# Linear attention and two experts on one core: inputs asked for earlier, finer dependencies in the plan, other buffers, another seam

## The chip, the cores and the metric

The kernel runs on one core of a Trainium2 chip. The metric is the device time of one execution in microseconds (us). Names: PE is TensorE, DVE is VectorE, ACT is ScalarE, POOL is GpSimd, SP is SyncE, whose queue issues the DMAs.

## What is computed

```python
def _attn_ref(q, k, v):                      # 4 x 8 heads x 768 x 64
    gamma = 1.0 - 2.0 ** (-5.0 - np.arange(H))
    for t in range(S):
        state = gamma * state + einsum('bhd,bhe->bhde', k[:, :, t], v[:, :, t])
        y[:, :, t] = scale * einsum('bhd,bhde->bhe', q[:, :, t], state)
# x: [3072, 512], the heads side by side
def _moe_ref(x, w_in, w_out, g_ln):          # 512 -> 1024 -> 512
    h = x @ w_in
    solu = h * softmax(h)
    return (layer_norm(solu) * g_ln) @ w_out
def _moe2_ref(x, w_in, w_out):               # 512 -> 2048 -> 512
    h = x @ w_in
    return (h * np.cos(h)) @ w_out
```

The weights come as 64-bit numbers and are turned into float32 on the chip. Nearly every product is made of three matmuls, because each operand is split into a high and a low part (high*high, high*low, low*high).

## The kernel before

**Plan and order.** `Body.record` doesn't issue instructions. It records operations with `Plan.add`: an engine, an estimated cost, a function that issues, keys that are read (`r`) and written (`w`), and a bias. An operation's due time is the PE work recorded before it, plus the bias. `Plan.order` then simulates the engines by these costs and keys. PE takes its operations in recorded order or out of a short look-ahead; DVE, ACT and POOL take the ready one that is due first; SP takes a ready one among the next 16 in due order that are due within `SP_WIN` = 10 us of the first (lines 180 and 181). A DMA's end is taken from its size over `MBUS` plus `LAND`. The order in which the simulation starts them is the order in which every engine's instructions are issued; on the chip each engine works through its own list in order. Two operations that write one key are put one behind the other by the plan, with the landing of a DMA between them, also where the tiles behind the key are different ones.

**Stage 1, to about 387 us.** 24 attention steps, each 64 tokens of two batches, each with one block of small 64x64 matmuls: scores of step n + 1 (`sc`, L325), the state (`S`, L333) and the outputs of step n (`y`, L346). `load` (L285) brings a step's inputs by two DMAs, `dk` (L292) and `sv` (L296), into three buffers each. `attend` in `record` records the load of step n + 1 ahead of the block with outputs n. Between the steps stand the first expert's matmuls: `mm1` (L603) with `norm`, then for groups of 512 tokens `transp` (L665) into two PSUM banks, whose high and low parts ACT and DVE write (`lth`, `ltl`), and `mm2` (L697). One unit of `mm2` is 24 matmuls into one bank; ACT copies the bank to `ys` (L708, one buffer), and SP stores that to DRAM (`y1d`, L713). The last `HOLD` = 2 units of the first five groups are kept back until the attention is over.

Beside this, `keep` prepares the second expert's weights in 16 blocks: raw words are fetched into one buffer (`raw0`, L422), ACT and DVE turn them (`words`, L429 to L449), ACT and DVE write high and low parts into one buffer `big`, and SP stores these to DRAM (`cbd`, L586, and `o2d`, L538).

**Seam, about 369 to 416 us.** The held units, then `SEAM`, an order written out by hand: the last group's transposes (`t:`), its `mm2` units in parts (`m:d:a:b`), and the first products of the second expert (`P:`). `load_y` fetches `y1d`, forms sums and writes high and low parts to `Y`; half 0 at step `Y_AT`, half 1 behind the attention.

**Stage 2, to the end.** Three superblocks of 1024 tokens. Each has a first loop of eight steps (7 products, L867, with weights `cb` in three slots, and the previous step's part of the output matmuls `acc`, L973) and a second loop of eight steps with `acc` alone. A product goes through `wave` (six ACT and DVE operations, cosine among them, `ki` in two buffers) to a `G`. Each of the 16 steps takes one pair of weight pieces `o2` (L808, 512 KB each), in three slots; the pair for step k + 3 is asked for behind step k. At the end of each loop `leave` copies four banks and issues eight output stores (L1003). `load_cb(q + 3)` is recorded behind the products of step q; `load_y(s + 1)` between the two loops. The buffers for Y's raw sums (`yts`) lie in part in the tile that the products' ACT copies use too.

Of the kernel before, what the change touches and what calls it, by code (L numbers as in the profile page):

```python
# [33 lines left out]
NS = NB2 * NI  # L34
# [3 lines left out]
HOLD = 2  # L38
NU = 10
RING = 4  # L40
# [11 lines left out]
MBUS = 0.40  # L52
EASE = 0.08
FETCH = 3.4
BACKLOG = 5.0
WARM = 28
V_ACT = (0, 1, 3, 4, 5, 6, 7)
LAND = 2.0
# [14 lines left out]
JOIN = 2  # L73
Y_AT = 21
B_YLOAD = 0.0
# [9 lines left out]
SEAM = ("t:0 t:1 P:1 P:2 t:2 t:3 P:5 t:4 t:5 P:6 m:0:0:1 t:6 t:7 P:7 m:0:1:3 P:4 m:0:3:4 P:3"  # L85
        " m:1:0:4 m:2:0:4 m:3:0:4")
# [24 lines left out]
class Plan:  # L111
# [115 lines left out]
class Body:  # L227
# [121 lines left out]
    def attn(self, scores=None, outs=None, look=1):  # L349
# [7 lines left out]
        if outs is not None:  # L357
# [8 lines left out]
            if i:  # L366
                r += [("s", n % 2), ("dk", n % 3)]
# [17 lines left out]
        if carry:  # L385
            def copy():
                s = self.new("att", ("s", n + 1), [128, 8, D], F32, f"s{(n + 1) % 2}")
                self.nc.scalar.activation(out=s, in_=self.t["S", self.steps[n][0]], func=AF.Copy)
            self.add("ACT", 0.62, copy, r=[("S",)], w=[("s", (n + 1) % 2)])
# [111 lines left out]
    def keep(self, what):  # L501
# [11 lines left out]
        rk, wk = self.words(what, src, "stg", 0, False, early=EARLIER)  # L513
# [13 lines left out]
        if not wk_in:  # L527
# [13 lines left out]
            for l in range(2):  # L541
                self.add("SP", 0.4, lambda l=l: store(l), r=[("big",), ("big", l)], w=[("o2d", it, l)], mb=0.524, bias=b + B_STORE)
# [38 lines left out]
        for i in range(2):  # L581
# [5 lines left out]
            self.add("SP", 0.4, store, r=[("big",)] + [("big", m) for m in range(3)], w=[("cbd", 2 * c + i, e)], mb=0.459, bias=b + B_STORE)  # L587
# [130 lines left out]
    def load_y(self, s, es=(0, 1)):  # L718
        T, nc = self.t, self.nc
        for e in es:  # L720
# [11 lines left out]

            def yt(e=e):
                return T["yts", e]

            def fetch(m, e=e, yt=yt):
# [5 lines left out]
            def split(k, a, b, x, y, old=[], e=e, tile=tile, pools=pools, yt=yt):  # L742
# [13 lines left out]
                r = [("yt", e, i) for i in range(x, y)]  # L756
                self.add("ACT", 1.10 if b - a > 1 else 0.62, high, r=r + pools, w=[k, (*k, a)] + old, bias=B_YMIX)
                self.add("DVE", 1.25 if b - a > 1 else 0.70, low, r=r, w=[k, (*k, a)], bias=B_YMIX, name="two")
            for m in range(2):
                self.add("SP", 0.4, lambda m=m, fetch=fetch: fetch(m), r=[("y1d", 2 * s + m, 2 * e + i) for i in range(2)] + pools,  # L760
                         w=[("yt", e, 2 * m), ("yt", e, 2 * m + 1)], mb=0.524, bias=B_YLOAD)
# [3 lines left out]
            for to, x, y in ((0, 2, 0), (2, 3, 2), (3, 3, 0), (1, 1, 3)):  # L765
                self.add("DVE", 0.70, mix(to, x, y), r=[("yt", e, x), ("yt", e, y)], w=[("yt", e, to)], bias=B_YMIX, name="two")
# [3 lines left out]
    def load_cb(self, q):  # L770
# [21 lines left out]
        if sl != 1:  # L792
            self.add("SP", 0.5, fetch, r=r, w=[("cb", sl)] + old, mb=1.835, bias=B_CB)
        else:
            for e in range(2):
                for l in range(2):
                    self.add("SP", 0.4, lambda e=e, l=l: fetch(e, l), r=r, w=[("cb", sl)] + (old if not e + l else []),
                             mb=0.459, bias=B_CB)

    def load_o2(self, k):  # L800
# [8 lines left out]
        for l in range(2):  # L809
            self.add("SP", 0.4, lambda l=l: fetch(l), r=[("o2d", it, l)],  # L810
                     w=[("o2", sl)] + ([("u", 8), ("u", 9)] if k == 0 and l == 0 else []), mb=0.524, bias=B_O2)

    def rooms(self):
# [3 lines left out]
        def stg():  # L817
            T["yts", 1] = self.p["stg"].tile([128, 4, 512], F32, tag="raw0", name="yts")
            T["kis"] = self.p["stg"].tile([128, 2, 512], I32, tag="wt0", name="kis")
        self.add("CTL", 0.0, stg, w=[("raw", "stg", 0), ("wt", "stg", 0), ("ki", 0), ("ki", 1)] + [("yt", 1, i) for i in range(4)])  # L820
# [9 lines left out]
    def room0(self):  # L830
        T = self.t

        def sb():
            t = self.new("sb", ("yts", 0), [128, 4, 512], F32, "yts0")
            for i in range(1, 4):
                T["t", i] = t[:, i]
        self.add("CTL", 0.0, sb, r=[("pool", "sb")], w=[("yt", 0, i) for i in range(4)])
# [15 lines left out]
    def product(self, q, which):  # L853
# [18 lines left out]
        self.add("PE", 1.36, go, r=need + [("cb", q % 3)], w=[key], name=f"P{which} {q}", ni=12)  # L872
# [4 lines left out]
        def plus(dst, i, src):  # L877
            def put():
                nc.vector.tensor_tensor(out=T["t", 1] if dst[0] == "yt" else T[dst], in0=T["t", i], in1=T[src], op=ALU.add)  # L879
            return put  # L880
        if which in "167":
            i = {"1": 1, "6": 2, "7": 3}[which]
            self.add("ACT", 0.62, copy(i), r=[key], w=[("yt", 0, i)], bias=B_POST)
        if which == "2":
            self.add("DVE", 0.70, plus(("yt", 0, 1), 1, ("W",)), r=[("W",)], w=[("yt", 0, 1)], bias=B_POST)
            self.wave(q, ("yt", 0, 1), None, True)
        if which == "7":
            self.add("DVE", 0.70, plus(("hs", 2 * it + 1), 3, ("Z",)), r=[("yt", 0, 3), ("Z",)], w=[("hs", 2 * it + 1)], bias=B_POST)
# [3 lines left out]
        if which == "3":  # L892
            self.add("DVE", 0.70, plus(("hs", 2 * it), 2, ("Z",)), r=[("yt", 0, 2), ("Z",)], w=[("hs", 2 * it)], bias=B_POST)
            self.wave(q, ("hs", 2 * it), None, False)

    def wave(self, q, hk, _, near):
# [3 lines left out]
        ks = n % 2  # L900
        kk = ("ki", ks)
        h = lambda: T["t", 1] if hk[0] == "yt" else T[hk]
        ki = lambda: T["kis"][:, ks]
# [55 lines left out]
    def parts(self, n, k, which, c, first=False, last=False, stop=False):  # L959
# [3 lines left out]
        for j in range(2):  # L963
            gs = which[j]
            for t in range(4):
# [10 lines left out]
                def put(j=j, gs=gs, t=t, go=go):  # L976
                    self.add("PE", 0.68, go, r=[("G", gs), ("o2", k % 3), ("pool", "psacc")],
# [10 lines left out]
    def leave(self, n, t):  # L988
# [10 lines left out]
        for b in range(2):  # L999
# [4 lines left out]
            self.add("SP", 0.4, store, r=[("o", t, 0), ("o", t, 1)], mb=0.131)  # L1004
# [31 lines left out]
    def record(self):  # L1036
# [7 lines left out]
        def attend():  # L1044
# [4 lines left out]
            if n + 1 < NS and ("L", n + 1) not in self.used:  # L1049
                self.load(n + 1)  # L1050
# [106 lines left out]
        for s in range(NSUP):  # L1157
            for it in range(8):
# [100 lines left out]
```

## Time and profile before

| | us |
|---|---|
| runs | 909.59, 909.13, 903.25 (median 909.13) |
| profiled execution | 915.32 |
| its span, first to last instruction | 913.5 |

The span is cut into stretches below: attention and first expert to 387 us, seam to 416 us, then the second expert. A `dk<-kq_dram` is a DMA from `kq_dram` to `dk`.

### The profile page before, as it was taken

The numbers are of one execution on the slowest core, as the hardware profiler recorded it, in microseconds if no ns is written. First come the engines' busy times: TensorE is split into PE (matmuls) and PEld (weight loads), VectorE is DVE, ScalarE is ACT, GpSimd is POOL, SyncE is SP. The second block draws the span as 40 slices with busy tenths as digits, with TensorE's granted clock in tenths as the row PEclk, the third lists the DMA queues.
The fourth block names the chain that finished last, engine by engine and source line by source line (L and its number), as shares of the span: only waits on it lengthen the run. The fifth ranks groups of instructions, "written<-read, shape, count | busy, mean of one in ns | idle before, by whom it ended". The sixth has DMA issues, their size and how long they took to land.

```text
span 913.5 us, 15993 instructions
## 1 busy us (share of the span) xinstructions
PE 866.0 (95%) x6504; PEld 711.8 (78%) x6504; DVE 643.1 (70%) x993; ACT 467.6 (51%) x746; POOL 89.6 (10%) x193
## 2 busy tenths in 40 slices
PE   7899999988996998999999989999998999999997
PEld 6688877877775876787888868888886888888876
DVE  6777887776875697554878871697889348878721
ACT  4577664644654466443555641565555226555521
POOL 0034331221231122000000000000000000000000
PEclk8989999999997999999999999999999999999999
DMA  9754726676777455658464875654669546642373
GB/s 352 246 175 153 256 86 237 249 248 248 256 271 260 158 188 196 249 159 296 153 233 152 299 256 187 212 179 165 222 213 333 173 140 227 220 160 93 121 237 103
DMA packets 48042, 190.90 MB, mean 209 GB/s; under 512 B 5472, under 2 KB 5472, under 8 KB 45920
## 3 DMA queue, kind: packets, MB, share of 16 engines
q1 hardware_dynamic: 47824, 189.81, 59.4%
q8 instruction: 51, 0.84, 0.4%
q14 instruction: 23, 0.19, 0.1%
q10 hardware_dynamic: 144, 0.06, 0.0%
HBM read 154.20 MB, written 35.65 MB: 208 GB/s over the span
## 4 chain that ended last, share of the span: by engine, by line
PE 74%; DMA 12%; DVE 6%; ACT 3%; issue 2%; POOL 1%; SPq 1%; ACTq 0%; DVEq 0%; POOLq 0%
PE acc L973 26%; PE X L867 14%; PE h L603 10%; PE Z L867 7%; DMA dk<-kq_dram 6%; PE y L697 5%; PE W L867 3%; PE y L346 2%; DMA o<-o2d 2%; PE sc L325 2%; PE h L697 2%; PE S L333 1%; PE tr L665 1%; DVE sm L621 1%; DVE big L568 1%
## 5 line engine op out<-in xcount | busy, mean ns | idle before, releaser
L973 PE MATMUL acc<-o,G 128*128 128x512 f32 x768 | 187.6, 395 | 4.8 <-DMA o<-o2d 4.8
L973 PEld LDWEIGHTS acc<-o,G 128*128 128x128 f32 x768 | 146.2, 191 | 37.0 <-DMA o<-o2d 5.6
L603 PE MATMUL h<-w,xh 128*128 128x512 f32 x384 | 131.9, 411 | 3.9 <-ACT xh L402 2.0
L973 PE MATMUL acc<-o2u,G 128*128 128x512 f32 x384 | 93.7, 390 | 2.0 <-DMA o2u<-o2d 2.0
L603 PEld LDWEIGHTS h<-w,xh 128*128 128x128 f32 x384 | 75.1, 196 | 22.5 <-ACT xh L402 2.2
L973 PEld LDWEIGHTS acc<-o2u,G 128*128 128x128 f32 x384 | 71.9, 188 | 17.7 <-DMA o2u<-o2d 2.8
L603 PE MATMUL h<-w,xl 128*128 128x512 f32 x192 | 78.1, 407 | 0.6 <-DVE xl L406 0.6
L927 ACT ACTIVATE rs<-rs,hp 128x512 f32<-128x512 f32 x96 | 68.8, 718 | 15.7 <-DVE rs L924 15.3
L875 ACT ACTIVATE yts<-X 128x512 f32<-128x512 f32 x72 | 43.1, 598 | 62.8 <-PE X L867 62.8
L697 PE MATMUL y<-lth,o1h 128*128 128x512 f32 x168 | 68.5, 408 | 5.2 <-ACT ys L708 5.2
L955 DVE TENSOR_TENSOR G<-hs,G 128x512 fp32r<-128x512 f32 x48 | 32.6, 692 | 51.2 <-ACT G L952 51.1
L697 PE MATMUL y<-ltl,o1h 128*128 128x512 f32 x168 | 66.5, 396 | 0.4 <-DVE ltl L676 0.4
L921 DVE SCALAR_TENSOR_TENSOR rs<-kis,rs 128x512 f32<-128x512 int32 x96 | 66.1, 688 | 0.8
L879 DVE TENSOR_TENSOR yts<-yts,W 128x512 f32<-128x512 f32 x24 | 16.5, 688 | 71.2 <-PE W L867 71.2
L697 PE MATMUL y<-lth,o1l 128*128 128x512 f32 x168 | 66.3, 395 | 0.0
L952 ACT ACTIVATE G<-hs 128x512 fp32r<-128x512 f32 x48 | 30.2, 630 | 70.1 <-PE acc L973 68.6
L915 ACT ACTIVATE kis<-hs 128x512 int32<-128x512 f32 x48 | 30.4, 633 | 37.8 <-DVE hs L879 36.4
L867 PE MATMUL X<-Y,cbu 128*128 128x512 f32 x192 | 48.9, 390 | 0.7 <-ACT ys L708 0.7
L867 PE MATMUL X<-Y,big 128*128 128x512 f32 x192 | 49.1, 391 | 0.0
L867 PE MATMUL X<-Y,cb 128*128 128x512 f32 x192 | 48.7, 389 | 0.0
L325 PEld LDWEIGHTS sc<-dk 64*64 64x64 f32 x768 | 27.3, 146 | 22.2 <-issue 13.3
L603 PEld LDWEIGHTS h<-w,xl 128*128 128x128 f32 x192 | 38.0, 198 | 8.2 <-DVE xl L406 0.9
(110 smaller groups left out, 1693.5 us busy)
## 6 DMA issues: line engine op xcount, KB each, us to landing
o<-o2d SPq DMA_DIRECT2D x64, 512.0 KB, 4.8
o2u<-o2d SPq DMA_DIRECT2D x32, 512.0 KB, 4.8
sv<-vk_dram SPq DMA_DIRECT2D x24, 640.0 KB, 7.0
cbd<-big SPq DMA_DIRECT2D x16, 896.0 KB, 5.1
big<-cbd SPq DMA_DIRECT2D x8, 1792.0 KB, 8.3
cbu<-cbd SPq DMA_DIRECT2D x32, 448.0 KB, 6.2
cb<-cbd SPq DMA_DIRECT2D x8, 1792.0 KB, 7.9
dk<-kq_dram SPq DMA_DIRECT2D x24, 512.0 KB, 6.2
```

The costliest lines, as they stand in the source:

```text
L325: self.nc.tensor.matmul(out=sc[r, j], lhsT=dk[r, 0, j], rhs=dk[r, 1, j], start=True, stop=True)
L346: self.nc.tensor.matmul(out=self.t["y", n][self.half[1 - p], j], lhsT=lhs, rhs=rhs, start=(intra and j == 0), stop=(j == 7 and last), skip ...
L603: self.nc.tensor.matmul(out=h[:, c], lhsT=a[:, k], rhs=self.w1s[k // 2][:, l, k % 2, cs], start=(k + m == 0), stop=(k == KD - 1 and m == 2))
L697: self.nc.tensor.matmul(out=self.t["y1", g, d], lhsT=w[:, j, ds], rhs=a, start=(j + m == 0), stop=(j == K1 - 1 and m == 2))
L867: nc.tensor.matmul(out=out, lhsT=w[i][:, a], rhs=y[b][:, j], start=(start and m == 0), stop=(m == 5), skip_group_check=True)
L875: return lambda: nc.scalar.activation(out=T["t", i], in_=T[key], func=AF.Copy)
L915: nc.scalar.activation(out=ki(), in_=h(), func=AF.Identity, scale=INV2PI, bias=0.25)
L921: nc.vector.scalar_tensor_tensor(out=r(), in0=ki(), scalar=-C2, in1=r(), op0=ALU.mult, op1=ALU.add)
L927: nc.scalar.activation(out=r(), in_=r(), func=AF.Sin, bias=self.hp[:, 0:1])
L952: nc.scalar.activation(out=T["G", gs][:, 0], in_=g(), func=AF.Copy)
L955: nc.vector.tensor_tensor(out=T["G", gs][:, 1], in0=g(), in1=T["G", gs][:, 0].bitcast(F32), op=ALU.subtract)
L973: nc.tensor.matmul(out=T["acc", n, t], lhsT=a[:, ts_], rhs=w, start=(first and j == 0 and m == 0), stop=(last and j == 1 and m == 2))
```

## The change

- `load` of step n + 2 is recorded at step n, from step n = 6 (`AHEAD`) on; before, that of step n + 1 at every step.
- Keys by piece: the two halves of an `o2` pair and the four pieces of a `cb` block have keys of their own.
- Raw words in `keep` take turns in two buffers (`raw0`, `raw2`), and Y's raw sums use these too. `t1` to `t3` are tiles of their own, `ki` has one buffer (before two), the state copy `s` one (two), `x` three (four); the scratch for dynamic DMAs is 512 (4096).
- Three `mm2` units are held (two). `SEAM` has the transposes and the last group's first unit ahead of the products.
- The raw sums of Y for the next superblock are fetched at step 5 of the first loop, the rest of `load_y` at step 0 of the second loop. One `cb` load moves from step 7 of the first loop to step 6 of the second.
- In the simulation: `MBUS` 0.37 (0.40), a `LEAD` of 1.2 before the transfer, `LAND` 1.3 (2.0), `BACKLOG` 6.5 (5.0); from 45 us on, SP looks at 24 operations in a window of 40 us (16 in 10 us), a DMA issued by SP ends 1 us (`SLACK`) later, and the stores of `cbd`, `o2d` and the output, named "lax", count as ready 1 us later.

```diff
-HOLD = 2
+HOLD = 3
-RING = 4
+RING = 3
-MBUS = 0.40
+MBUS = 0.37
-BACKLOG = 5.0
+BACKLOG = 6.5
-LAND = 2.0
+LEAD = 1.2
+LAND = 1.3
+AHEAD = 6
+SLACK = 1.0
+SLACK_FROM = 45.0
+SP_WIN2 = 40.0
-SEAM = ("t:0 t:1 P:1 P:2 t:2 t:3 P:5 t:4 t:5 P:6 m:0:0:1 t:6 t:7 P:7 m:0:1:3 P:4 m:0:3:4 P:3"
-        " m:1:0:4 m:2:0:4 m:3:0:4")
+SEAM = ("t:0 t:1 t:2 t:3 m:0:0:1 t:4 t:5 m:0:1:2 t:6 t:7 m:0:2:4 m:1:0:2 P:1 P:2 m:1:2:4 P:5 P:6"
+        " m:2:0:2 P:7 m:2:2:4 P:4 m:3:0:2 P:3 m:3:2:4")
...
-                    cand = [i for i in sp[sat:sat + 16 + stuck] if not left[i] and not done[i]
-                            and (stuck or ops[i][7] <= ops[sp[sat]][7] + SP_WIN)]
+                    cand = [i for i in sp[sat:sat + 24 + stuck] if not left[i] and not done[i]
+                            and (stuck or ops[i][7] <= ops[sp[sat]][7] + (SP_WIN if free["SP"] < SLACK_FROM else SP_WIN2))]
...
-                wire = max(wire, end) + ops[i][4] / MBUS
+                wire = max(wire, end + LEAD) + ops[i][4] / MBUS
                 end = wire + LAND
+                if ops[i][0] == "SP" and start > SLACK_FROM:
+                    end += SLACK
             for s in succ[i]:
...
+                if ops[s][0] == "SP" and ops[s][6] == "lax" and start > SLACK_FROM:
+                    hop += SLACK
...
-        rk, wk = self.words(what, src, "stg", 0, False, early=EARLIER)
+        n = self.used["keep"] = self.used.get("keep", -1) + 1
+        rk, wk = self.words(what, src, "stg", n % 2 * 2, False, early=EARLIER)
...
-    def load_y(self, s, es=(0, 1)):
+    def load_y(self, s, es=(0, 1), fetched=True, made=True):
...
+            if s == 0:
+                n = self.used["keep"] = self.used["keep"] + 1
+                keys = [("raw", "stg", n % 2 * 2)] * 4
+            else:
+                n = 1 - e
+                keys = [("yt", e, i) for i in range(4)]
...
-            self.add("SP", 0.5, fetch, r=r, w=[("cb", sl)] + old, mb=1.835, bias=B_CB)
+            self.add("SP", 0.5, fetch, r=r, w=[("cb", sl, i) for i in range(4)] + old, mb=1.835, bias=B_CB)
...
-                     w=[("o2", sl)] + ([("u", 8), ("u", 9)] if k == 0 and l == 0 else []), mb=0.524, bias=B_O2)
+                     w=[("o2", sl, l)] + ([("u", 8 + l)] if k == 0 else []), mb=0.524, bias=B_O2)
...
-            if n + 1 < NS and ("L", n + 1) not in self.used:
-                self.load(n + 1)
+            for m in (n + 1, n + 2)[:1 if n < AHEAD else 2]:
+                if m < NS and ("L", m) not in self.used:
+                    self.load(m)
...
-                if q + 3 < 8 * NSUP and q >= 0:
+                if it < 7 and q + 3 < 8 * NSUP:
                     self.load_cb(q + 3)
+                if it == 5 and s + 1 < NSUP:
+                    self.load_y(s + 1, made=False)
...
-            if s + 1 < NSUP:
-                self.load_y(s + 1)
             for it in range(8):
+                if s + 1 < NSUP and it == 0:
+                    self.load_y(s + 1, fetched=False)
+                if s + 1 < NSUP and it == 6:
+                    self.load_cb(8 * s + 10)
```

## Rows read from the trace of the kernel before

**Rows 1.** The line of the core; then the page's first part (busy us, share).
```profile
core 0: 913.5 us, clock 0.974
...
PE 866.0 (95%) x6504; PEld 711.8 (78%) x6504; DVE 643.1 (70%) x993; ACT 467.6 (51%) x746; POOL 89.6 (10%) x193
```

**Rows 2.** PE's waits from 105 to 387 us: total us, times, longest.
```profile
PE sc L325 <- DMA dk<-kq_dram: 12.6, 6, 4.7
PE y L697 <- ACT ys L708: 5.2, 4, 3.1
PE y L346 <- issue: 3.3, 1, 3.3
PE tr L665 <- DVE ltl L676: 2.1, 3, 0.9
PE h L603 <- DVE u L627: 1.5, 2, 1.1
```

**Rows 3.** PE's waits from 387 us to the end.
```profile
PE acc L973 <- DMA o<-o2d: 4.8, 2, 2.6
PE acc L973 <- DMA o2u<-o2d: 2.0, 2, 1.1
```

**Rows 4.** Stretches: length, then PE, PEld, DVE, ACT, POOL busy; clock, DMA share, GB/s.
```profile
145.00:300.00 155.00, 136.81 (x1538) 112.95 (x1536) 110.34 (x148) 80.36 (x119) 34.24 (x67) 0.92 0.70 254
...
300.00:350.00 50.00, 48.52 (x291) 40.22 (x290) 42.61 (x60) 30.72 (x46) 11.35 (x21) 1.00 0.55 200
...
416.00:516.00 100.00, 99.67 (x439) 82.39 (x440) 78.45 (x137) 53.50 (x89) 0.00 (x0) 1.00 0.61 217
```

**Rows 5.** The same view, of the seven stretches at half clock behind 105 us.
```profile
217.70:221.11 3.41, 3.24 (x119) 3.27 (x123) 1.54 (x2) 0.73 (x1) 1.04 (x1) 0.50 1.00 400
285.96:299.61 13.65, 9.05 (x140) 7.71 (x141) 3.30 (x4) 3.32 (x4) 1.04 (x1) 0.50 0.61 231
361.06:364.47 3.41, 3.41 (x10) 2.63 (x9) 2.91 (x3) 1.02 (x2) 0.00 (x0) 0.50 0.22 82
...
sum 34.11, PE 29.34 PEld 25.08 DVE 15.45 ACT 6.89 POOL 5.01; mean PE 4.19 PEld 3.58 DVE 2.21 ACT 0.98 POOL 0.72
```

**Rows 6.** PE's timeline around 364 us: start, duration.
```profile
362.12 0.63 PE L697 MATMUL y<-lth,o1l 128*128 128x512 f32 x1
362.55 0.63 PE L697 MATMUL y<-ltl,o1h 128*128 128x512 f32 x1
...
364.59 0.39 PE L697 MATMUL y<-lth,o1l 128*128 128x512 f32 x1
364.82 0.39 PE L697 MATMUL y<-ltl,o1h 128*128 128x512 f32 x1
```

**Rows 7.** SP's timeline from 145 us; SP's waits; the page's DMA issues (us to landing).
```profile
145.59 0.80 SPq L586 DMA_DIRECT2D cbd<-big  x2
...
147.47 1.20 SPq L292 DMA_DIRECT2D dk<-kq_dram  x1
...
SPq L586 <- DVE big L568: 53.8, 8, 12.1
...
dk<-kq_dram SPq DMA_DIRECT2D x24, 512.0 KB, 6.2
```

**Rows 8.** ACT's timeline at 359 us: start, duration, idle before and its releaser.
```profile
358.94 1.12 ACT L429 ACTIVATE wt<-raw 128x1024 f32<-128x1024 f32 x1 [1.91 <-DMA raw<-w_out_dram]
359.96 0.59 ACT L708 ACTIVATE ys<-y 128x512 f32<-128x512 f32 x1
```

**Rows 9.** SP's timeline from 526 us: start, duration.
```profile
526.54 3.10 SPq L1003 DMA_DIRECT2D out_dram<-o  x5
...
530.32 1.75 SPq L1003 DMA_DIRECT2D out_dram<-o  x3
532.17 2.08 SPq L808 DMA_DIRECT2D o<-o2d  x4
```

**Rows 10.** SP's waits over the whole run.
```profile
SPq L292 <- PE y L346: 60.6, 11, 11.1
```

More of the change, by code (lines that the diff above doesn't have):

```diff
@@ L386, in copy @@
             def copy():
-                s = self.new("att", ("s", n + 1), [128, 8, D], F32, f"s{(n + 1) % 2}")
+                s = self.new("att", ("s", n + 1), [128, 8, D], F32, "s0")
                 self.nc.scalar.activation(out=s, in_=self.t["S", self.steps[n][0]], func=AF.Copy)
-            self.add("ACT", 0.62, copy, r=[("S",)], w=[("s", (n + 1) % 2)])
+            self.add("ACT", 0.62, copy, r=[("S",)], w=[("s",)])
         def out():
@@ L541, in keep @@
             for l in range(2):
-                self.add("SP", 0.4, lambda l=l: store(l), r=[("big",), ("big", l)], w=[("o2d", it, l)], mb=0.524, bias=b + B_STORE)
+                self.add("SP", 0.4, lambda l=l: store(l), r=[("big",), ("big", l)], w=[("o2d", it, l)], mb=0.524, bias=b + B_STORE, name="lax")
             return
@@ L586, in store @@
                 self.nc.sync.dma_start(out=T["cbd", it][:, e], in_=T["qs", what][:, i].bitcast(F32))
-            self.add("SP", 0.4, store, r=[("big",)] + [("big", m) for m in range(3)], w=[("cbd", 2 * c + i, e)], mb=0.459, bias=b + B_STORE)
+            self.add("SP", 0.4, store, r=[("big",)] + [("big", m) for m in range(3)], w=[("cbd", 2 * c + i, e)], mb=0.459, bias=b + B_STORE, name="lax")
     def mm1(self, n, c, parts=((0, 1, 2, 3),), passes=(0, 3), look=1, done=True):
@@ L731, in tile, with fetch @@
                 T["Y2", e] = y
+            if s == 0:
[4 more added lines that the diff above has]
+                keys = [("yt", e, i) for i in range(4)]
             def yt(e=e):
                 return T["yts", e]
-            def fetch(m, e=e, yt=yt):
+            def fetch(m, e=e, yt=yt, n=n):
+                if s == 0 and m == 0 or ("yts", e, 1) not in T and s:
+                    self.new("stg", ("yts", e), [128, 4, 512], F32, f"raw{n % 2 * 2}")
+                    T["yts", e, min(s, 1)] = True
                 nc.sync.dma_start(out=yt()[:, 2 * m:2 * m + 2], in_=T["y1d", 2 * s + m][:, 2 * e:2 * e + 2])
@@ L755, in low @@
                     nc.vector.tensor_tensor(out=half(1), in0=src(), in1=half(0).bitcast(F32), op=ALU.subtract)
-                r = [("yt", e, i) for i in range(x, y)]
+                r = [keys[i] for i in range(x, y)]
                 self.add("ACT", 1.10 if b - a > 1 else 0.62, high, r=r + pools, w=[k, (*k, a)] + old, bias=B_YMIX)
                 self.add("DVE", 1.25 if b - a > 1 else 0.70, low, r=r, w=[k, (*k, a)], bias=B_YMIX, name="two")
-            for m in range(2):
+            for m in range(2 if fetched else 0):
                 self.add("SP", 0.4, lambda m=m, fetch=fetch: fetch(m), r=[("y1d", 2 * s + m, 2 * e + i) for i in range(2)] + pools,
-                         w=[("yt", e, 2 * m), ("yt", e, 2 * m + 1)], mb=0.524, bias=B_YLOAD)
+                         w=keys[2 * m:2 * m + 1 + (s > 0)], mb=0.524, bias=B_YLOAD)
+            if not made:
+                continue
             yk = ("Yt", e)
@@ L765, in load_y @@
             for to, x, y in ((0, 2, 0), (2, 3, 2), (3, 3, 0), (1, 1, 3)):
-                self.add("DVE", 0.70, mix(to, x, y), r=[("yt", e, x), ("yt", e, y)], w=[("yt", e, to)], bias=B_YMIX, name="two")
+                self.add("DVE", 0.70, mix(to, x, y), r=[keys[x], keys[y]], w=[keys[to]], bias=B_YMIX, name="two")
             split(yk, 3, 5, 0, 2)
@@ L796, in load_cb @@
                 for l in range(2):
-                    self.add("SP", 0.4, lambda e=e, l=l: fetch(e, l), r=r, w=[("cb", sl)] + (old if not e + l else []),
+                    self.add("SP", 0.4, lambda e=e, l=l: fetch(e, l), r=r, w=[("cb", sl, 2 * e + l)] + old[2 * e + l:2 * e + l + 1],
                              mb=0.459, bias=B_CB)
@@ L817, in stg @@
         def stg():
-            T["yts", 1] = self.p["stg"].tile([128, 4, 512], F32, tag="raw0", name="yts")
-            T["kis"] = self.p["stg"].tile([128, 2, 512], I32, tag="wt0", name="kis")
-        self.add("CTL", 0.0, stg, w=[("raw", "stg", 0), ("wt", "stg", 0), ("ki", 0), ("ki", 1)] + [("yt", 1, i) for i in range(4)])
+            t = self.p["stg"].tile([128, 2, 512], I32, tag="wt0", name="kis")
+            T["kis"], T["t", 3] = t[:, 0], t[:, 1].bitcast(F32)
+        self.add("CTL", 0.0, stg, w=[("wt", "stg", 0), ("ki",), ("t", 3)])
         def us():
@@ L833, in sb @@
         def sb():
[L834 to L837, printed above, removed]
+            for i in (1, 2):
+                self.new("sb", ("t", i), [128, 512], F32, f"t{i}")
+        self.add("CTL", 0.0, sb, r=[("pool", "sb")], w=[("t", 1), ("t", 2)])
     def rooms2(self):
@@ L871, in product @@
         need += [(k, e, {0: 0, 1: 0, 2: 2, 3: 3, 4: 3, 5: 5, 6: 5}[b]) for k, e in need]
-        self.add("PE", 1.36, go, r=need + [("cb", q % 3)], w=[key], name=f"P{which} {q}", ni=12)
+        self.add("PE", 1.36, go, r=need + [("cb", q % 3, i) for i in range(4)], w=[key], name=f"P{which} {q}", ni=12)
         def copy(i):
@@ L878, in put @@
             def put():
-                nc.vector.tensor_tensor(out=T["t", 1] if dst[0] == "yt" else T[dst], in0=T["t", i], in1=T[src], op=ALU.add)
+                nc.vector.tensor_tensor(out=T["t", 1] if dst[0] == "t" else T[dst], in0=T["t", i], in1=T[src], op=ALU.add)
             return put
@@ L882, in product @@
             i = {"1": 1, "6": 2, "7": 3}[which]
-            self.add("ACT", 0.62, copy(i), r=[key], w=[("yt", 0, i)], bias=B_POST)
+            self.add("ACT", 0.62, copy(i), r=[key], w=[("t", i)], bias=B_POST)
         if which == "2":
-            self.add("DVE", 0.70, plus(("yt", 0, 1), 1, ("W",)), r=[("W",)], w=[("yt", 0, 1)], bias=B_POST)
-            self.wave(q, ("yt", 0, 1), None, True)
+            self.add("DVE", 0.70, plus(("t", 1), 1, ("W",)), r=[("W",)], w=[("t", 1)], bias=B_POST)
+            self.wave(q, ("t", 1), None, True)
         if which == "7":
-            self.add("DVE", 0.70, plus(("hs", 2 * it + 1), 3, ("Z",)), r=[("yt", 0, 3), ("Z",)], w=[("hs", 2 * it + 1)], bias=B_POST)
+            self.add("DVE", 0.70, plus(("hs", 2 * it + 1), 3, ("Z",)), r=[("t", 3), ("Z",)], w=[("hs", 2 * it + 1)], bias=B_POST)
             self.wave(q, ("hs", 2 * it + 1), None, False)
@@ L892, in product @@
         if which == "3":
-            self.add("DVE", 0.70, plus(("hs", 2 * it), 2, ("Z",)), r=[("yt", 0, 2), ("Z",)], w=[("hs", 2 * it)], bias=B_POST)
+            self.add("DVE", 0.70, plus(("hs", 2 * it), 2, ("Z",)), r=[("t", 2), ("Z",)], w=[("hs", 2 * it)], bias=B_POST)
             self.wave(q, ("hs", 2 * it), None, False)
@@ L899, in wave @@
         n = self.used["wave"] = self.used.get("wave", -1) + 1
[L900 to L903, printed above, removed]
+        kk = ("ki",)
+        h = lambda: T["t", 1] if hk[0] == "t" else T[hk]
+        ki = lambda: T["kis"]
         m = n % 2 if n < 4 else n % 4
@@ L976, in put @@
                 def put(j=j, gs=gs, t=t, go=go):
-                    self.add("PE", 0.68, go, r=[("G", gs), ("o2", k % 3), ("pool", "psacc")],
+                    self.add("PE", 0.68, go, r=[("G", gs), ("o2", k % 3, 0), ("o2", k % 3, 1), ("pool", "psacc")],
                              w=[("acc", t)], name=f"down {n},{k},{j},{t}", ni=6)
@@ L1003, in store @@
                 nc.sync.dma_start(out=self.a["out"][row:row + C], in_=T["o", n, t][b * C:(b + 1) * C])
-            self.add("SP", 0.4, store, r=[("o", t, 0), ("o", t, 1)], mb=0.131)
+            self.add("SP", 0.4, store, r=[("o", t, 0), ("o", t, 1)], mb=0.131, name="lax")
     def setup(self):
```

6 lines of the change are left out of this document (3 added, 3 removed).

## The prediction

> **What bounds the kernel now.** I read the views from the widest to the narrowest. The line of the core and the page's first part [rows 1] say that TensorE (PE) is busy for 95% of a span of 913.5 us, at a mean granted clock of 0.974. So the end is set by PE; what can be gained is what it waits plus what it loses while its clock is down. Second, PE's waits by stage. From 105 to 387 us (the first expert's matmuls beside the attention steps and the preparation of the second expert's weights) they are [rows 2]: 12.6 us for the attention input dk, 5.2 for ACT's copy ys, 3.3 "issue", 2.1 and 1.5 for DVE. From 387 us to the end only the streamed weights o2 count: 4.8 + 2.0 us [rows 3]. The wait shown begins at the modelled end of the matmul before, so the sums below are slightly low. Third, three stretches [rows 4]: from 416 to 516 us PE is busy 99.67 of 100 us beside a DVE at 78%; from 300 to 350 it loses 1.5 of 50 us beside a DVE at 85%; from 145 to 300 it is busy only 136.81 of 155 us, at a granted clock of 0.92, with the DMA engines at 0.70. The time to be had lies in the last of these.
>
> **The clock.** Behind every long wait a stretch follows in which the granted clock is 0.50, that is 1.2 and not 2.4 GHz. Seven of them lie behind 105 us and sum to 34.11 us; three are shown [rows 5], and the four not shown (at 156.26, 200.63, 541.96 and 705.80) last 3.41 us each like two of these. Inside one, 128x512 matmuls start 0.43 us apart, after it 0.23 us [rows 6]. So a stretch of 3.41 us loses 1.7 us of work. Before each of them PE stood for 2 us or more.
>
> **Term 1: attention inputs two steps ahead (from step 6 on), with SP's order.** SyncE (SP) issues in order. At 145.59 us it issues two stores cbd that stand for the end of DVE's work on a weight block, and dk follows only at 147.47; over the run SP stands 53.8 us for such stores, 8 times, 12.1 us at the longest [rows 7]. A dk takes 6.2 us to land (median, same group), and PE stands for it six times: 12.6 us [rows 2]. In the changed kernel the dk and sv of step n+2 are recorded where those of n+1 were. Their buffers (three) come free when the attention block of the step before has run, so one whole step, 242/14 = 17 us, lies between a free buffer and the place where the load stood before. Against a landing of 6 to 8 us that covers the wait with some 9 us to spare. Bounds: nothing, if SP still puts them behind the stores; 12.6 us of waits, if all go. I take 12.6, since 17 is far over 8. With them go the clock stretches behind three of the waits, 3 x 1.7 = 5.1 us. The fourth, 13.65 us from 285.96, holds the issue wait too and only 9.05 us of PE work, half of which is lost: 4.5 us. I leave 1.7 of it with the issue wait and take 2.8. Together 20.5 us.
>
> The loads are no more than before, two DMAs a step. What is queued behind them on SP (raw words, cbd, y1d) waits two issues longer, under 3 us, only where they come first.
>
> **Term 2: two buffers of raw words, three held units.** At 357 us PE stands 3.1 us for ys, the copy that empties the one PSUM bank of the second matmul. ACT is in order: ahead of that copy it holds the first step of a weight block, which begins only when its raw words have landed, at 358.94 [rows 8]. Raw words had one buffer and so were asked for only when the block before was done. With two they are there before; the wait and its stretch of half clock go: 3.1 + 1.7. The other three waits on ys (5.2 - 3.1 = 2.1 us) are units that follow each other in the same bank, and a copy between them: they stay, except the one ahead of the held units (0.7 us), because three held units alternate between two banks from the first on. Bounds 0.7 (only that) to 6.9 (all and the stretch); taken 5.5.
>
> **Term 3: streamed weights by piece, stores marked lax, Y and cb loads moved out of the burst.** At 526.54 SP begins eight output stores, 3.10 + 1.75 us of issuing, and four o2 loads stand behind them until 532.17 [rows 9]. PE needs a new o2 pair every 24 matmuls, 24 x 0.23 = 5.5 us there. PE stands 4.8 + 2.0 us for such loads in the three loops of that kind [rows 3], and in two of them the clock falls: 3.4 us. In the plan, the second half of a pair no longer waits for the landing of the first, stores count as ready 1 us later, and SP may choose over a window of 40 us instead of 10, so that loads go ahead of stores. The four Y loads of the next superblock leave at the sixth step of the loop before, and one block of cb at the seventh step of this loop. Bounds 0 to 10.2; taken 8, since the eight stores still have to be issued somewhere in the same loop.
>
> **What is added or hidden.** (a) As the stage from 145 to 300 us shrinks to about 135 us, DVE's 110.34 us in it [rows 4] rise from 71 to 82%. The stretch from 300 to 350, at 85%, loses 3% of PE, so I charge 4 us; bounds 0 and 8. (b) In the seam the eight transposes and the last group's second matmul now come first, the products later. The transposes have two banks, and each waits for DVE to empty one; the longest such wait is 0.9 us [rows 2]. Bounds 0 and 7 (eight of them); I take 2, because the six matmuls put between two pairs cover most of it. (c) One buffer for ki instead of two makes ACT wait for DVE in each of 96 chains; from 416 to 516 us PE loses 0.33 us beside a DVE at 78% [rows 4], and the results are wanted a product step later. Taken 0; bounds 0 and the 3% of a DVE at 85%, some 14 us over that whole part. (d) Three x and one s buffer: s is read by the block that ends with writing S, x is read a step before its buffer is asked for again. Taken 0, bound 0.6 us a step. (e) Issue waits: 3.3 us [rows 2], left as they are, with 1.7 us of clock; they may go or double.
>
> Of (e) a page of the Trainium skill says otherwise: Runtime: NRT & Kernel Launch, section on instruction fetch mechanics, has the cost of a new block of code "mostly hidden". By that rule such a wait would not come back and the time would be 5 us lower; the trace has the 3.3 us, though it does not name what the sequencer lacked, so I keep it.
>
> **Sum.** 20.5 + 5.5 + 8 = 34 us gone, 4 + 2 = 6 us added: 28 us less. From the profiled execution's own 915.3 us that gives 887; from the median of the runs shown, 909.1, it gives 881. The profiled execution is 5.7 us above the slowest of those runs. If it is longer because its waits are, the end doesn't depend on that, and 887 is right; if the profile itself costs time, 881. I take 884.
>
> **Rivals.**
> 1. New waits eat half the gain. For it: the DMA engines already run full in places (388 to 400 GB/s, 0.96 to 1.00 busy, as in the stretch at 217.70 [rows 5]), the mean of 254 GB/s from 145 to 300 us would rise to 292, and DVE to 82%. Against it: dk then has some 9 us to spare. Two more waits of the size of the issue wait, each with its clock (2 x 5 us), and twice the charge on DVE (4 us) make 14 us: 884 + 14 = 898.
> 2. The loads don't come earlier: SP's order still holds them behind stores, term 1 is nothing, the others remain: 34 - 20.5 - 6 = 7.5 us less, 902 to 908 by the two bases; 905. Against it: nothing but the order holds them now.
> 3. Slower: the loads that were sent ahead park SP. They wait for the attention block of the step before; whatever is behind them on SP waits too, the store of y1d above all, and without it the single ys cannot be rewritten and PE stops at the next unit. For it: SP already stands 60.6 us in front of L292 for PE's attention block, 11 times, 11.1 us at the longest [rows 10]. Between two units lie 242/17 = 14.2 us; less a landing of 6.2 (that of dk, the nearest row) that leaves 8 us. Below 8 us of parking it costs nothing (the mean is 5.5); at the 11.1 it costs 3.1 + 1.7 = 4.8 us a step. On ten of the fourteen steps: 48 - 28 = 20 us slower, 929. Against it: the order is laid out by a plan that issues a load only when its buffer is expected free, and all of those 11 waits are of the early steps, where PE hardly notices.
> The Trainium skill (DMA: Bandwidth & Descriptors, on the anatomy of a DMA) has every semaphore wait on the issuing sequencer, ahead of the dispatch, which is what this rival needs; the trace agrees by the 60.6 us.
>
> **How the numbers follow.** Forecast 0.62, its own range 871 to 895; rival 1 0.22; rival 2 0.09; rival 3 0.07. A measurement of this kernel tells about 1% from no change, so faster means below 900, slower above 918. Faster: 0.62 + two thirds of rival 1 + a little of rival 2 = 0.80. Same: the rest of these, 0.13. Slower: 0.07. Low end: all waits of rows 2 and 3 and half of the PE work in the slow stretches gone, 24.7 + 6.8 + 14.7 = 46 us, is 863; I put 866. High end: it takes in rival 1 and the start of rival 2: 903.
>
> **What would show it.** Right: no PE wait for dk behind 105 us, the dk issued over 10 us before it is used; ACT not waiting for raw words; no o2 wait over 1 us where the output stores are; a granted clock of about 0.985. Wrong in a step: dk waits left (term 1), SP standing at L292 in the later steps with waits on ys beside it (rival 3), transposes waiting over 1 us each in the seam (b), products waiting for G (c). Wrong as a whole: a span at or over 900 us, or PE waits that add up to the same under other names.

## The result, and the profile after

The changed kernel takes 874.57 us (median of 4 runs, 873.90 to 875.99) where the kernel before, timed beside it, takes 909.36: a ratio of 0.963, 95% interval 0.958 to 0.968. It is faster. The forecast was 884 us, in a range of 866 to 903.

The line of the core:

```profile
core 0: 872.1 us, clock 0.992
```

From the page, one of the DMA issues (median us to landing):

```profile
dk<-kq_dram SPq DMA_DIRECT2D x24, 512.0 KB, 4.1
```

The span is 41.4 us shorter than in [rows 1], the clock 0.992 for 0.974. PE runs the same 6504 matmuls; it waits less and runs less of them at half clock. Its waits from 105 to 360 us, and from there to the end (total us, times, longest), answer to [rows 2] and [rows 3]:

```profile
PE tr L675 <- DVE ltl L686: 1.7, 2, 1.0
PE h L613 <- DVE u L637: 1.6, 2, 1.0
PE y L707 <- DVE ltl L686: 0.3, 1, 0.3
...
PE X L888 <- ACT t L896: 1.9, 1, 1.9
PE acc L993 <- DVE G L975: 1.7, 2, 0.8
PE X L888 <- ACT ys L718: 0.7, 1, 0.7
```

No DMA is left in either list. In stage 1, the 24.7 us of [rows 2] and 0.4 more have become 3.6; behind it, 6.8 us for o2 are gone, and 3.6 us of others are new: PE waits for a copy `t` by ACT and for `G` by DVE. (The 0.7 us for `ys` stood there before.) The stretches that answer to [rows 4] (length; PE, PEld, DVE, ACT, POOL busy; clock, DMA share, GB/s):

```profile
145.00:300.00 155.00, 152.39 (x1604) 126.05 (x1597) 123.62 (x170) 94.35 (x139) 39.52 (x77) 1.00 0.70 244
300.00:350.00 50.00, 49.02 (x241) 40.36 (x240) 42.06 (x56) 31.65 (x45) 9.50 (x16) 1.00 0.72 263
390.00:490.00 100.00, 98.13 (x433) 80.96 (x432) 83.76 (x145) 56.52 (x91) 0.00 (x0) 1.00 0.61 229
```

In the first, PE is busy 152.39 of 155 us where it was 136.81, at the full clock, with DVE at 80%. The DMA share there is the 0.70 it was. ACT, which stood 5.8 us for raw words in five waits of stage 1, has no such wait left. Of the seven stretches at half clock behind 105 us [rows 5] none is left up to the end of the matmuls; the two ahead of 105 us remain, the second of them shorter (3.41 us, before 6.83).

SP's timeline from 143 us (start, duration) answers to [rows 7]:

```profile
145.16 0.33 SPq L301 DMA_DIRECT2D dk<-kq_dram  x1
...
149.51 0.80 SPq L596 DMA_DIRECT2D cbd<-big  x2
```

SP's waits from 105 to 360 us answer to [rows 7] and [rows 10]:

```profile
SPq L301 <- PE y L355: 29.3, 8, 7.5
SPq L596 <- DVE big L578: 24.0, 7, 8.9
```

The dk now leaves ahead of the cbd stores and lands in 4.1 us instead of 6.2. And SP does stand in front of it, 8 times in this stage, for the attention block that frees its buffer, at the longest 7.5 us.

By the same view, from 495 us on, of the output stores [rows 9]:

```profile
495.67 0.32 SPq L830 DMA_DIRECT2D o<-o2d  x1
496.08 5.05 SPq L1023 DMA_DIRECT2D out_dram<-o  x8
501.24 1.75 SPq L830 DMA_DIRECT2D o<-o2d  x3
```

The stores still stand ahead of three o2 loads, and yet PE waits for none.

### The profile page after: what moved, and what is told of

It is laid out like the page before. It is cut to its first block, busy times and chain, and to the rows that moved or that the text cites. A ratio compares the mean times of both kernels' runs of the same rounds, so it can differ in the third digit from the quotient of the medians.

```text
span 872.1 us, 16015 instructions
## 1 busy us (share of the span) xinstructions
PE 847.5 (97%) x6504; PEld 700.2 (80%) x6504; DVE 642.9 (74%) x993; ACT 469.3 (54%) x746; POOL 96.4 (11%) x193
## 4 chain that ended last, share of the span: by engine, by line
PE 87%; DVE 6%; DMA 3%; issue 2%; ACT 1%; POOL 1%; SPq 0%; DVEq 0%; ACTq 0%; POOLq 0%
PE acc L993 28%; PE X L888 15%; PE h L613 14%; PE y L707 10%; PE Z L888 7%; PE W L888 4%; PE h L707 2%; PE sc L334 2%; PE tr L675 2%; PE S L342 1%; PE y L355 1%; DMA sv<-vk_dram 1%; PE h L291 1%; DMA cbd<-big 1%; DMA o2d<-big 1%
## 5 line engine op out<-in xcount | busy, mean ns | idle before, releaser
L993 PE MATMUL acc<-o,G 128*128 128x512 f32 x768 | 183.9, 389 | 1.7 <-DVE G L975 1.7
L993 PEld LDWEIGHTS acc<-o,G 128*128 128x128 f32 x768 | 144.0, 188 | 32.4 <-DVE G L975 2.5
L613 PE MATMUL h<-w,xh 128*128 128x512 f32 x384 | 129.0, 403 | 4.4 <-ACT xh L411 2.4
L613 PEld LDWEIGHTS h<-w,xh 128*128 128x128 f32 x384 | 73.2, 191 | 21.6 <-ACT xh L411 2.5
L707 PE MATMUL y<-lth,o1h 128*128 128x512 f32 x160 | 64.2, 401 | 0.0
L707 PE MATMUL y<-ltl,o1h 128*128 128x512 f32 x160 | 62.6, 391 | 0.3 <-DVE ltl L686 0.3
L707 PE MATMUL y<-lth,o1l 128*128 128x512 f32 x160 | 62.3, 389 | 0.0
L900 DVE TENSOR_TENSOR t<-t,W 128x512 f32<-128x512 f32 x24 | 16.5, 687 | 56.6 <-PE W L888 56.5
L896 ACT ACTIVATE t<-X 128x512 f32<-128x512 f32 x48 | 28.6, 596 | 45.4 <-PE X L888 45.1
L888 PEld LDWEIGHTS X<-Y,cb 128*128 128x128 f32 x192 | 36.0, 188 | 9.7 <-ACT t L896 2.3
```

The source lines that it names most:

```text
L613: self.nc.tensor.matmul(out=h[:, c], lhsT=a[:, k], rhs=self.w1s[k // 2][:, l, k % 2, cs], start=(k + m == 0), stop=(k == KD - 1 and m == 2))
L707: self.nc.tensor.matmul(out=self.t["y1", g, d], lhsT=w[:, j, ds], rhs=a, start=(j + m == 0), stop=(j == K1 - 1 and m == 2))
L888: nc.tensor.matmul(out=out, lhsT=w[i][:, a], rhs=y[b][:, j], start=(start and m == 0), stop=(m == 5), skip_group_check=True)
L896: return lambda: nc.scalar.activation(out=T["t", i], in_=T[key], func=AF.Copy)
L993: nc.tensor.matmul(out=T["acc", n, t], lhsT=a[:, ts_], rhs=w, start=(first and j == 0 and m == 0), stop=(last and j == 1 and m == 2))
```

## The experiments

Parts were undone one at a time in the changed kernel, two were tried alone in the kernel before, then more than one undone together. The kernels were timed in four groups, each on one chip beside the kernel before, whose medians there were 909.36, 908.70, 906.11 and 909.35 us. The changed kernel itself was timed in the first group alone. What a part is "worth" below is the difference from its 874.57 us, so it is taken across chips; the medians of the kernel before differ by 3.3 us between the groups, and a worth of that size is not told from nothing. Not undone by themselves were the tiles of `t1` to `t3`, the buffers of `s` and `x`, and the scratch.

**One step ahead again.**

```diff
-AHEAD = 6
+AHEAD = 99
```

> The changed kernel with the attention inputs of step n + 1 recorded at step n throughout, as before; everything else changed. Theory A (the earlier request itself removes the waits for dk): the six waits for dk behind 105 us come back, 12.6 us and some 8 us of half clock, so 875 + 20 = 895 us. Theory B (the new order of SP removes them, stores go behind loads and a wider window): no wait for dk over 1 us, 874 to 880 us.

877.32 us (876.76 to 879.08), ratio 0.966 (0.961 to 0.971), and no wait for dk in stage 1. Taken by itself the earlier request is worth 2.7 us here, no more than the groups differ by. That is what theory B said.

**SP's choice as before.**

```diff
-                    cand = [i for i in sp[sat:sat + 24 + stuck] if not left[i] and not done[i]
-                            and (stuck or ops[i][7] <= ops[sp[sat]][7] + (SP_WIN if free["SP"] < SLACK_FROM else SP_WIN2))]
+                    cand = [i for i in sp[sat:sat + 16 + stuck] if not left[i] and not done[i]
+                            and (stuck or ops[i][7] <= ops[sp[sat]][7] + SP_WIN)]
-SLACK = 1.0
+SLACK = 0.0
```

> The changed kernel with SP's choice in the plan as before: 16 operations in a window of 10 us, no slack behind DMAs and lax stores; two steps ahead stays. Theory A: dk still comes early, the waits for o2 behind the output stores come back in part (up to 10 us with the clock), so 876 to 886 us. Theory B: the waits for dk and those for o2 both come back, 895 us or more.

879.78 us (879.41 to 881.13), ratio 0.969 (0.964 to 0.974). No wait for dk, and 0.2 us for o2: worth 5.2 us by itself. Theory A had the time right, but the o2 waits that it named did not come back, so they stay away without the "lax" stores. Each of the two runs fits a theory that the other denies: with the new order alone dk is in time, and with the earlier request alone it is too.

**Each alone in the kernel before.** The same edits, put into the kernel before.

> The kernel before with the loads of step n + 2 recorded at step n from step 6 on, nothing else. Theory A: the waits for dk behind 105 us go, 909 - 20 = 889 us, the waits for ys and o2 stay. Theory B: SP's window holds the loads where they stood, 903 to 909 us, dk waits as before.

904.53 us (899.10 to 913.51 over 10 runs), ratio 0.995 (0.992 to 0.999).

> The kernel before with SP's new choice in the plan (24 operations in a window of 40 us, 1 us of slack behind SP's DMAs and for lax stores), nothing else. Theory A: the o2 waits shrink, dk waits stay: 897 to 903 us. Theory B: the dk waits go too: 880 to 889 us.

904.09 us (897.33 to 909.60 over 10 runs), ratio 0.997 (0.994 to 1.000). Neither is worth anything like 20 us; by the medians they give 4.2 and 4.6 us, and the second interval includes a ratio of 1. PE's waits from 105 to 387 us, first of the kernel with the earlier request, then of the one with SP's choice:

```profile
PE y L698 <- ACT ys L709: 6.8, 3, 5.5
PE tr L666 <- DVE ltl L677: 6.8, 8, 1.7
PE sc L326 <- DMA dk<-kq_dram: 5.2, 4, 3.1
PE X L868 <- DMA big<-cbd: 2.2, 1, 2.2
```

```profile
PE X L874 <- DMA big<-cbd: 13.4, 1, 13.4
PE y L704 <- ACT ys L715: 2.3, 3, 0.9
PE tr L672 <- DVE ltl L683: 2.2, 4, 1.0
```

In the first, SP still issues dk behind two cbd stores, as in [rows 7], and it lands in 6.0 us (median; before 6.2):

```profile
142.85 0.80 SPq L587 DMA_DIRECT2D cbd<-big  x2
143.75 0.88 SPq L293 DMA_DIRECT2D dk<-kq_dram  x1
```

In the second dk lands in 4.3 us, the wait for it is gone altogether from this stage, and stage 1 is over sooner: the last mm1 matmul ends 31.7 us earlier than in the profiled execution of before (317.8 for 349.5 us). But then PE stands 13.4 us in front of the first product, for `big<-cbd`, the first block of the second expert's weights, and the clock is at half for 13.65 us, from 352.22 us on. That product starts at 362.57 us, before at 380.50, so 13.8 of the 31.7 us are given back by then: the block goes into `big`, which is free only when the last of the 16 weight blocks has been stored. With stage 1 shorter, the preparation of the weights is late next. This was not among my rivals. It gave theory C. The two profiled executions lie 18.0 us apart where the medians lie 4.6 us apart (this one is the fastest of its ten, that of before was slower than the runs timed with it), so these traces don't show how much is given back in a usual execution.

**Raw words in one buffer again.**

```diff
-        rk, wk = self.words(what, src, "stg", n % 2 * 2, False, early=EARLIER)
+        rk, wk = self.words(what, src, "stg", 0, False, early=EARLIER)
...
-                n = self.used["keep"] = self.used["keep"] + 1
+                n = 1
```

> The changed kernel with the raw words of all weight blocks in one buffer again (Y's raw sums keep the other). Theory A (the second buffer only frees ACT for ys): one long ys wait comes back, 3 us and its clock, 878 to 880 us, first product where it was. Theory C (with stage 1 shortened, the chain of weight blocks ends last before the seam, and the second buffer shortens it): the last store of the blocks comes 5 to 15 us later than at 339 us, and the first product waits for the first cb block: 880 to 890 us.

891.40 us (890.77 to 891.88), ratio 0.988 (0.979 to 0.996): with 16.8 us the dearest single part. PE's waits from 105 to 400 us:

```profile
PE X L888 <- DMA big<-cbd: 12.4, 1, 12.4
PE tr L675 <- DVE ltl L686: 3.4, 5, 1.1
PE y L707 <- ACT ys L718: 0.7, 1, 0.7
```

SP's timeline at the end of the weight blocks:

```profile
358.19 0.62 SPq L548 DMA_DIRECT2D o2d<-big  x1
...
366.11 0.32 SPq L806 DMA_DIRECT2D big<-cbd  x1
```

The last store of a weight block is issued at 358.19 us, and the first cb load at 366.11; in the changed kernel the last two stores are issued from 338.73 us on and that load at 343.13. The last mm1 ends at 320.9 us as it does there (321.2). So the second buffer does nothing for the end of mm1; its worth lies in the weight blocks being done when PE comes for them, 12.4 us of waiting and a stretch of half clock, 13.7 us long, that begins in it. Theory C holds by its mechanism, though the stores come some 19 us later, not 5 to 15, and the time is 1.4 us beyond its range. Theory A falls: the long ys wait did not return. In the changed kernel, by SP's timeline, the raw words of the last two blocks are asked for together:

```profile
311.78 1.52 SPq L431 DMA_DIRECT2D raw<-w_out_dram  x2
```

**The old seam.**

```diff
-HOLD = 3
+HOLD = 2
...
-SEAM = ("t:0 t:1 t:2 t:3 m:0:0:1 t:4 t:5 m:0:1:2 t:6 t:7 m:0:2:4 m:1:0:2 P:1 P:2 m:1:2:4 P:5 P:6"
+SEAM = ("t:0 t:1 P:1 P:2 t:2 t:3 P:5 t:4 t:5 P:6 m:0:0:1 t:6 t:7 P:7 m:0:1:3 P:4 m:0:3:4 P:3"
...
```

> The changed kernel with two held units and the old order of the seam (products behind two transposes). Theory A (the new seam costs 2 us of waits for transposes, the old hid them): 871 to 875 us. Theory C (the products would now come before the first cb block has landed): PE waits 8 to 14 us for big<-cbd at the first product, with a clock stretch behind it: 884 to 893 us.

880.35 us (877.91 to 882.38), ratio 0.975 (0.967 to 0.984). Neither theory: it costs 5.8 us, but no wait for cb. PE's waits from 105 to 400 us:

```profile
PE y L707 <- ACT ys L718: 3.2, 2, 2.4
PE tr L675 <- DVE ltl L686: 2.0, 2, 1.1
```

The ys waits ahead of the hand-written order are back, and between 326 and 340 us there are two stretches of half clock of 3.41 us each. ACT comes late to the copy `ys` because an operation of the first expert ahead of it waits for POOL:

```profile
334.93 1.24 ACT L659 ACTIVATE u<-u,sm 128x1024 f32<-128x1024 f32 x1 [2.91 <-POOL sm L656]
336.08 0.58 ACT L718 ACTIVATE ys<-y 128x512 f32<-128x512 f32 x1
```

With the second raw buffer in place the cb block has landed in time even for the old order. The held units and the order were undone together, so what either is worth alone is not shown.

**Whole keys.** One key again for both halves of an o2 pair and for the four pieces of a cb block.

> The changed kernel with one key again for both halves of an o2 pair and for the four pieces of a cb block. If the keys are what removed the o2 waits: two or three waits for o2 of 1 to 3 us where the eight output stores are, two clock stretches, 881 to 885 us. If the moved loads or the lax stores did it: 873 to 877 us.

881.68 us (881.44 to 883.38), ratio 0.977 (0.966 to 0.987), worth 7.1 us. PE's waits from 390 us on:

```profile
PE acc L993 <- DMA o<-o2d: 3.7, 4, 2.0
PE X L888 <- ACT t L896: 1.9, 1, 1.9
PE acc L993 <- DVE G L975: 1.6, 2, 0.8
PE acc L993 <- DMA o2u<-o2d: 0.5, 2, 0.3
```

SP's timeline ahead of the first of these waits, which ends at 512.88 us:

```profile
499.37 0.32 SPq L830 DMA_DIRECT2D o<-o2d  x1
499.78 5.04 SPq L1023 DMA_DIRECT2D out_dram<-o  x8
504.87 0.58 SPq L811 DMA_DIRECT2D cbu<-cbd  x1
505.55 0.87 SPq L830 DMA_DIRECT2D o<-o2d  x2
```

With one key, the plan believes that a half or a piece must wait for the landing of the one before, though they go into different tiles. So the pieces of cb leave one by one, and the last goes out behind the stores and ahead of the o2 loads. In the changed kernel the four pieces leave together at 483.89 us, and the o2 loads follow the stores at once. There too the stores part the halves of a pair (495.67 and 501.24 us), and PE doesn't wait. The o2 waits are 4.2 of the 7.1 us; the two clock stretches that were expected did not come, and where the rest lies is not shown. Nor is it shown which of the two keys does it: they were undone together.

**The moved loads back.** Y's raw sums and the last cb block between the two loops again.

> The changed kernel with Y's raw sums fetched between the two loops again and the cb block of step 7 asked for there. If moving these loads out of the burst removed the o2 waits: waits for o2 of 2 to 3 us at the start of the first two second loops, 880 to 884 us. If the keys or the lax stores did it: 873 to 877 us.

875.23 us (874.87 to 876.17), ratio 0.970 (0.962 to 0.978), no wait for o2. With the keys by piece in place, moving these loads is worth nothing that can be measured.

**Both of the first two undone.** One step ahead and SP's choice of before.

> The changed kernel with both undone: inputs asked for one step ahead and SP's choice as before (16 operations, 10 us, no slack, no lax). If either of the two alone removes the waits for dk, so that each hid the other in the runs that undid one: dk waits behind 105 us come back, some 12 us and 8 us of clock, 890 to 896 us. If the second raw buffer removed them (SP no longer stands in front of the raw words): no dk wait over 1 us, 878 to 883 us.

895.86 us (891.34 to 899.06), ratio 0.985 (0.980 to 0.990): 21.3 us. By time, the first reading: either alone will do. By the waits from 105 to 400 us, not as I had put it:

```profile
PE tr L675 <- DVE ltl L686: 6.6, 7, 2.3
PE tr L675 <- issue: 4.3, 1, 4.3
PE y L707 <- ACT ys L718: 2.7, 2, 2.0
PE sc L334 <- DMA dk<-kq_dram: 2.0, 3, 1.2
```

Of the 12.6 us for dk only 2.0 come back. The rest is spread over DVE, ys and issue, with three stretches of half clock of 13.65 us together; the last mm1 ends 16.8 us later (338.0 for 321.2 us). Why DVE comes late there I didn't separate.

**Two parts alone.** SP's choice and the buffers stay; one step ahead, whole keys, the old seam, the loads between the loops, the DMA constants of before.

> The changed kernel with only SP's choice and the buffers kept (second raw buffer, one ki, s, three x); one step ahead, whole keys, old seam with two held units, loads between the loops, the DMA constants of before. If the parts add up: 875 + 3 + 6 + 7 + 1 = 892 us, with the last mm1 near 321 us. If they lean on each other: 897 to 905 us, with a wait for big<-cbd in the seam.

887.44 us (881.97 to 888.06), ratio 0.975 (0.971 to 0.979): a little better than the sum of the single losses. The last mm1 ends at 323.6 us, and no product waits for cb; the waits from 105 to 400 us are mostly for ys (6.0 us) and DVE (5.9). SP's choice, which alone gave 4.6 us, and the buffers with it give 909.35 - 887.44 = 21.9 of the 34.8 us.

**The DMA constants of before.**

```diff
-MBUS = 0.37
+MBUS = 0.40
-LEAD = 1.2
-LAND = 1.3
+LEAD = 0.0
+LAND = 2.0
-BACKLOG = 6.5
+BACKLOG = 5.0
```

> The changed kernel with the plan's DMA constants of before (MBUS 0.40, no LEAD, LAND 2.0, BACKLOG 5.0). If they only shift the order a little: 873 to 879 us, other small waits. If the plan's landing times decide where SP's loads stand: waits for DMAs in stage 1 of 2 us or more, 882 to 890 us.

879.15 us (877.96 to 880.58), ratio 0.967 (0.964 to 0.971). 4.6 us, just beyond the first case; in stage 1 the waits are for DVE and ys (one of 2.2 us, with a clock stretch of 3.41), none for a DMA. What of the constants does it, and whether another small shift of the order would cost as much, stays open.

**A try at a faster one: two ki buffers again.** `t3` gets a tile of its own; the room comes from two padding tiles, one cut from 120 to 8 columns and one of 48 columns taken away.

> The changed kernel with two ki buffers again and t3 in a tile of its own (room from two padding tiles); a try at a version below both. If the single ki makes the wait for ACT's copy t at the third product step (1.9 us): that wait goes, 871 to 873 us. If the wait has another cause: 874 to 876 us.

878.55 us (875.79 to 880.01, 6 runs), ratio 0.966 (0.963 to 0.969): not faster than the changed kernel. The changed kernel's ACT at its 1.9 us wait, then PE's waits of the kernel with two buffers from 360 us on:

```profile
397.47 0.63 ACT L935 ACTIVATE kis<-hs 128x512 int32<-128x512 f32 x1 [2.23 <-DVE rs L941]
...
398.62 0.57 ACT L896 ACTIVATE t<-X 128x512 f32<-128x512 f32 x1
```

```profile
PE X L888 <- ACT t L896: 1.0, 1, 1.0
PE X L888 <- ACT ys L718: 0.7, 1, 0.7
```

ACT stood 2.23 us for DVE's last read of the single ki, with the copy that PE needed behind. With two buffers that wait is 1.0, and those for G are gone: 2.6 us fewer waits. But the matmuls of the first loops come more slowly. PE's timeline near 430 us of the changed kernel, then of this one:

```profile
430.66 1.52 PE L888 MATMUL W<-Y,cbu 128*128 128x512 f32 x6
432.02 1.52 PE L888 MATMUL X<-Y,cbu 128*128 128x512 f32 x6
433.38 0.84 PE L993 MATMUL acc<-o,G 128*128 128x512 f32 x3
```

```profile
430.68 1.56 PE L888 MATMUL X<-Y,cbu 128*128 128x512 f32 x6
432.07 1.55 PE L888 MATMUL W<-Y,cbu 128*128 128x512 f32 x6
433.46 0.85 PE L888 MATMUL X<-Y,cbu 128*128 128x512 f32 x3
```

Twelve matmuls take 2.72 us in the one and 2.78 us in the other, at the full clock; the kernel with the old constants, timed on the same chip, has 1.36 us for six like the changed kernel (432.58 to 433.94 us). It is not all matmuls: from 425 to 475 us, with PE busy throughout, this kernel has 219 matmuls and the changed one 222, but the last 237 `acc` matmuls, without products between them, take 53.74 us here and 53.76 there. The edit also took away the padding, so tiles lie at other addresses. That this is the cause is not shown; a version with the room found elsewhere was not tried.

## Why the prediction was right, and where it wasn't

The direction, the bound (PE by its waits and its clock) and the size were right: 34.8 us less than the median of before, forecast 28 by that base. Against the profiled executions it is 41.4 us. The choice of 884 between two bases could have been made: the profiled execution of the changed kernel is the fastest of its four, so no cost of the profile shows, and executions of the kernel before go from 895.69 us at a granted clock of 0.988 to 915.69 at 0.977. The profiled 915.3 was one of the long ones, and by the prediction's own rule that makes 887. That the time falls into the range is in part luck: two of the three terms owe their size to something else than they say, and some of what was charged wasn't due.

**Term 1 (20.5 us).** With both of its halves undone the time rises by 21.3 us, which is the size of the term, but not by its account: of the 12.6 us of dk waits 2.0 return, the rest stands under other names, and why stays open. So that the two numbers agree is luck in part. The step that "nothing but the order holds them" was right: in the changed kernel either half alone keeps dk in time; in the kernel before, SP's choice alone does, and the earlier request alone leaves 5.2 us of dk waits: dk still goes out behind the stores there, the case in which the term put its lower bound. And alone, in the kernel before, neither half gives over 5 us. One reading was off without changing the sum: between 145 and 387 us the trace has eight score blocks, 18.8 us apart, not fourteen 17 us apart.

**Term 2 (5.5 us).** The mis-sized one. The second raw buffer is worth 16.8 us, three times the term with its held units, and for another reason than the step "the wait and its stretch of half clock go": with one buffer that wait did not return. I asked which PE waits it removes in the trace of before, and not what is late once term 1 is taken: the last weight block, and with it the first cb. With one buffer 12.4 us, and clock with them, would have been given back in the seam.

**Term 3 (8 us).** Size right: the keys are worth 7.1 us, 4.2 of them as waits for o2. The other two causes were not needed: without the lax stores 0.2 us of o2 waits are left and without the moved loads none, and in the kernel before SP's choice with lax stores leaves 7.4 us of them (5.8 + 1.6). The stores stand ahead of o2 loads as before; what the whole keys hold back until then made those loads late, as in the kernel before, where a piece of cb goes out between the eight stores (529.69 us).

**Added costs.** (a) 4 us for DVE: waits for DVE in stage 1 are 3.6 us as they were (2.1 + 1.5 in [rows 2]), at 80% busy. Not due. (b) 2 us for the seam: one wait of 1.0 us for DVE stands at the transposes there (at 346 us). The run with the old seam is 5.8 us slower, but by ys waits and clock that I had put under term 2; what the order alone is worth is not shown. (c) ki at nothing: 2.6 us of waits, by the run with two. (e) The issue wait of 3.3 us is gone with its clock, 5 us that I left in. But one of 4.4 us still stands at 41 us in the changed kernel, and one of 4.3 us at 177 us in the run with both halves of term 1 undone. The Trainium skill (Runtime: NRT & Kernel Launch, instruction fetch mechanics) calls the cost of a new block of code "mostly hidden". No trace here names what the sequencer lacked in these waits, so whether they are such a cost stays open. Of the 13.4 us by which the drop of 41.4 us exceeds the forecast 28, (a) and (e) are 9.

**Rivals.** Rival 1's denser engines did not bind: 0.70 DMA share and no DMA wait. Rival 2 fell by the waits: none for dk is left. Rival 3's parking is there, 8 times in stage 1 behind 105 us and up to 7.5 us; I had put the point from which it costs at 8 us, and no wait of PE for ys followed in that stage.

## What to carry to other kernels

Take the largest wait out on paper, and then ask what is late next: here the two cures for a 12.6 us wait gave under 5 us each in the kernel before; one of them together with new buffers, the second one in a side chain that PE did not wait for among them, gave 21.9. Undo parts in the new kernel as well as adding them to the old one: two cures for one wait each look nearly worthless when undone alone (2.7 and 5.2 us, together 21.3), and each looks so when added alone where a third part is missing. In a planned order, a key that covers two tiles makes the plan wait where nothing needs to; it then tears apart what could leave together.

## What was not expected of the hardware

Twelve 128x512 matmuls at the full clock took 2.78 us instead of 2.72, in the first loops alone, in a kernel with two ki buffers and tiles at other addresses, which ate 2.6 us of removed waits; the cause is open. And dk, at the same size, took 4.1 us to land instead of 6.2, with the mean DMA share from 145 to 300 us unchanged at 0.70. Asking earlier does not do that by itself: in the kernel before with the earlier request alone dk still went out behind two cbd stores (1.8 MB) and took 6.0 us; with SP's choice alone it took 4.3. So the place behind the stores is the likely reason; no run changed that alone.
